# Row-group transposes, a shared PSUM pool and a VectorE finish in an attention-plus-SoLU kernel

## The chip, the core and the metric

One core of a Trainium2 chip runs the kernel. The metric is device time in microseconds (us): the median of the runs, 1267.34 us before (three runs, 1265.64 to 1268.81). The engines are TensorE (PE, its weight loads PEld), VectorE (DVE), ScalarE (ACT), GpSimd (POOL) and SyncE (SP), which issues every DMA here. All arithmetic is fp32.

## The reference

`x` is 4 batches of 12608 tokens with 128 channels; 32 learned "inducing" points attend to it, and then the tokens attend to the result. The attention output goes token by token through a feed-forward layer of width 1024:

```
h   = softmax(scale * I @ x.T) @ x          # per batch: [32,128], pass 1
y   = softmax(scale * x @ h.T) @ h          # per batch: [12608,128], pass 2
u   = y @ w_in                              # [tokens,1024]
s   = u * softmax(u)                        # "SoLU"
out = ((s - mean(s)) / sqrt(var(s) + 1e-6) * g_ln) @ w_out
```

## The kernel before, in words

Tokens are cut into tiles of 128: 99 per batch, 396 in all. Three stages run per batch.

- **Pass 1** (`p1`, L529): groups of up to 12 tiles (`PG`, nine groups a batch) are loaded, transposed on PE (`turn4`, L571, in two halves per group), copied to `xT` by ACT (L557), stored to DRAM as `xd`, scored against the inducing points (L600), reduced and exponentiated, and gathered (L682). Batch 0 does this up front with PSUM banks of its own; the next batch's pass 1 is woven into the current batch's tiles.
- **Pass 2** (`p2`, L763): groups of up to 12 tiles (`AG`) are read back from `xd`, scored (L790), transposed by DVE (L797), reduced (L799), shifted on POOL (L802), exponentiated on ACT (L809) and copied once more on POOL (L810), so that the weights stand twice. They are summed (L814), negated on ACT (L815) and inverted (L816). PE turns the doubled weights, two tiles to a transpose (`turn4`, L826), and ACT copies them to `aT` (L834).
- **Feed-forward**, tile by tile (`main` L903, `soft` L952): `mm1` (L924) multiplies the weights of one tile by `hs` = h @ w_in; DVE normalises with the row extreme (L962); ACT takes the exponential (L972); POOL multiplies (L976); ACT squares with a sum (L987); DVE transposes 32x32 blocks into `vt` (L1000). When the four tiles of a group are turned, `products` (L1034) starts two streams of 32 steps (L1045).

A 32-row matmul uses one of four row groups of the array. `mm1` of tile `i` uses the pair of row groups `i % 2`, and a products stream `w` uses pair `w`. `beats` (L855) interleaves them: while one pair does `mm1`, the other takes steps of its stream. Transposes and scores use the whole array.

Each products stream fills a PSUM buffer `op` of its own (`OP[w]`, one per pair); `evacuate` (L1059) copies it to `raw` on DVE or ACT, whichever the planner takes (L1067). Everything else shares two buffers `H`. Per three groups (`FG`) `finish` (L1076) forms the variance and its inverse root: a square on ACT (L1088), three small POOL operations (L1091 to L1093), Ln and Exp on ACT (L1098, L1099), four small POOL operations (L1104 to L1107), and per group a scaling of `raw` into `os` on ACT (L1122, four instructions) or POOL (L1118), then the store (`stored`, L1129). `floor` (L1012) prepares each group's epsilon with two POOL operations (L1017, L1018) and deals it out by DMAs.

The order on every engine is fixed when the program is built. A `Planner` (L125) runs the stages as coroutines with an estimated cost for each operation and semaphore; an engine takes, among the operations ready within `SLACK`, the one with the lowest priority number, mostly the tile index `t` plus an offset (`PR_*`). A `Lock` (L112) hands out buffers.

Of the kernel before, what the change touches and what calls it, by code (L numbers as in the profile page):

```python
# [8 lines left out]
F32 = mybir.dt.float32  # L9
# [14 lines left out]
KC = FF // P  # L24
GS = 4
FG = 3
PG = 12
AG = 12
JB = FF // M
JC = 2  # L30
BEAT = 225
EAGER = 120
# [19 lines left out]
SPARES = 8  # L52
H_LAST = -30
HN_MORE = 4
# [4 lines left out]
P1_FROM = 5  # L59
P1_GO = -20  # L60
P1_STEP = 7
P2_AHEAD = 35
P2_START = 35
PR_EX = -4
PR_EV = -20
PR_FI = 20
PR_G2 = 4
PR_HN = 2
PR_MU = 1
PR_SQ = 1  # L70
PR_TU = 6
RUSH = -100.0
SLACK = {"PE": 0, "ACT": 200, "DVE": 300, "POOL": 0, "SP": 0}
SPARE = 150
WARM = 32
WOUT = -13.5
# [169 lines left out]
def set_attention_then_solu_kernel(ctx: ExitStack, tc: tile.TileContext, x, inducing, w_in, w_out, g_ln, out):  # L246
# [6 lines left out]
    p1_groups = cut(NT, PG, GS)  # L253
# [4 lines left out]
    NP, NG = len(p1_groups), len(ff_groups)  # L258
# [26 lines left out]
    def small(i, **widths):  # L285
# [20 lines left out]
    OP = [Lock(), Lock()]  # L306
# [3 lines left out]
    A4 = Lock([buf([P, AG * 2 * M], "a4")])  # L310
# [3 lines left out]
    os_b = bufs(2, [P, GS, C], "os")  # L314
    OS = Lock()
    ST = Lock([
        dict(qe=buf([P, GS, 2], f"qe{i}"), S=buf([P, GS], f"st{i}"), dd=dd_pool.tile([P * 2 * GS], F32, name=f"dd{i}")) for i in range(4)
# [9 lines left out]
    RUN = [dict(m=buf([P, NP], f"m{i}"), l=buf([P, NP], f"l{i}"), acc=buf([P, C], f"acc{i}")) for i in range(2)]  # L327
# [118 lines left out]
    def weights_out():  # L446
# [29 lines left out]
        for k in range(NP):  # L476
            yield p1_done[0][k]
# [38 lines left out]
    p1_done, l_done = ([[Event() for _ in range(NP)] for _ in range(NB)] for _ in range(2))  # L516
    chain = [[Event() for _ in range(NP + 1)] for _ in range(NB)]
    each = PG * C
    wc_flat = wc.rearrange("p j d -> p (j d)")
    EARLY_X = Lock([f[:, i * each : (i + 1) * each].rearrange("p (s c) -> p s c", c=C) for f, n in ((wc_flat, 2), (spare, SPARES * FF // each)) for i in range(n)] + xn_b)  # L520
    EARLY_T = Lock([vt_all[:, i * each : (i + 1) * each].rearrange("p (s t) -> p s t", t=P) for i in range(3 * GS * FF // each)] + [xT_b])
    e2 = [wc_flat[:, 2 * each : 2 * each + PG * M], wc_flat[:, 2 * each + PG * M : 2 * each + 2 * PG * M]] + [o.rearrange("p s c -> p (s c)")[:, : PG * M] for o in os_b]
    EARLY_EW = Lock([(e2[i], e2[i + 1].rearrange("p (s m) -> p s m", m=M)) for i in (0, 2)] + [ew_b])
# [3 lines left out]
    turned = [Event() for _ in range(NP)]  # L527

    def p1(b, k):  # L529
        s0, n = p1_groups[k]  # L530
# [34 lines left out]
        for c0 in range(0, n, most):  # L565
# [28 lines left out]
        sc = big[:, : PG * M]  # L594
        mq = big[:, 512 - C : 512 - C + 4]
# [121 lines left out]
    def combine(b):  # L717
        prev = yield l_done[b][NP - 1]
        mine = RUN[b % 2]
        l, acc = mine["l"][:, NP - 1 : NP], mine["acc"]  # L720
# [7 lines left out]
        prev = yield p1_done[b][NP - 1]  # L728
# [27 lines left out]
        for k in range(1 if b else 2):  # L756
            spawn(half(FF if b else 512), PRIO_P1(b, NP - 1) if b else -28)
# [5 lines left out]
    def p2(b, j):  # L763
# [4 lines left out]
        for k, (g0, gn) in enumerate(p1_groups):  # L768
# [39 lines left out]
        a2 = a4.rearrange("p (s r m) -> p s r m", r=2, m=M)  # L808
        de = yield Op("ACT", 90 + 27 * n, lambda: nc.scalar.activation(a2[:, :n, 0, :], s2[:, :n, :], AF.Exp, scale=scale), d, arel)  # L809
        dp = yield Op("POOL", 100 + 30 * n, lambda: nc.gpsimd.tensor_copy(a2[:, :n, 1, :], a2[:, :n, 0, :]), de)  # L810
# [3 lines left out]
        d = yield Op("DVE", 66 + 33.4 * n, lambda: nc.vector.tensor_reduce(out=nr[:, :n], in_=a2[:, :n, 0, :], op=ALU.add, axis=AX.X), de)  # L814
        d = yield Op("ACT", 100, lambda: nc.scalar.activation(nr[:, :n], nr[:, :n], AF.Copy, scale=-1.0, bias=-1e-9), d)  # L815
        dr = yield Op("DVE", 138, lambda: nc.vector.reciprocal(rn[:, :n], nr[:, :n]), d, rel)  # L816
        give(S2, (s2, mx, nr), dr)
        for q0 in range(0, -(-n // 2), 8):
            q1 = min(q0 + 8, -(-n // 2))
            tr, trel = yield bank  # L820
            wide = min(P, (n - 2 * (q1 - 1)) * 2 * M)

            def turn4():
                for q in range(q0, q1):
                    h = P if q < q1 - 1 else wide
                    nc.tensor.transpose(out=tr[:h, (q - q0) * P : (q - q0 + 1) * P], in_=a4[:, q * P : q * P + h], identity=ident)  # L826

            dt = yield Op("PE", SWITCH + 108.7 * (q1 - q0), turn4, dp, trel)
            dc = []
            for h, qa, qb in ((P, q0, q1 if wide == P else q1 - 1), (2 * M, q1 if wide == P else q1 - 1, q1)):  # L830
                if qb > qa:
                    d = yield Op(
                        "ACT", 94 + 96 * (qb - qa),
                        lambda: nc.scalar.copy(  # L834
                            aT[:h, qa:qb, :], tr[:h, (qa - q0) * P : (qb - q0) * P].rearrange("p (q t) -> p q t", t=P)
# [5 lines left out]
            for s in range(2 * q0, min(2 * q1, n)):  # L841
                plan.set(aT_ready[(b, s0 + s)], dr, *dc)
# [399 lines left out]
```

## Time and profile before

| | |
|---|---|
| runs | 1267.34, 1268.81, 1265.64 us |
| profiled execution, first to last instruction | 1265.6 us |
| TensorE clock granted, mean | 0.988 |
| DVE, ACT, POOL busy over the span | 89%, 90%, 87% |
| DMA queue 1 (all dynamic DMAs) | 28.1% of 16 engines, 108.62 MB |
| instructions | 75903 |

The span of the profiled execution equals the fastest of the runs and lies 1.7 us below their median. In the profile a line such as `L976 POOL TENSOR_TENSOR eu<-spare,eu` is a group of instructions by source line, engine and operand names; `x187` counts them, then come busy us and mean ns of one, then the idle time just before them. `PE` rows overlap: several 32-row matmuls are in the array at once, so 98% busy does not mean that all four row groups work. A windows row gives each engine's busy us and instruction count in a stretch.

### The profile page before, as it was taken

What the parts mean: (1) busy time and instruction counts of PE and PEld (TensorE: products, weight loads), DVE (VectorE), ACT (ScalarE), POOL (GpSimd) and SP (SyncE); (2) the same over time, 40 slices, a digit from 0 to 9 for tenths busy, and PEclk for the clock granted to TensorE, in tenths of its full rate; (3) what the DMA queues carried; (4) which work ended last, traced back from release to release, by engine and by line L of the source; (5) the groups of instructions that cost most, each with busy time, mean ns of one, the idle gap of its engine ahead of it and who ended that gap; (6) DMA issues with size and microseconds to landing.
All of it is one profiled execution on the core that took longest, in us unless ns stands there. A gap on an engine that the chain in (4) does not pass through costs nothing. (4 is left out here: it accounts for less than half of the span.)

```text
span 1265.6 us, 75903 instructions
## 1 busy us (share of the span) xinstructions
PE 1236.0 (98%) x34240; PEld 1127.8 (89%) x34240; DVE 1123.3 (89%) x1803; ACT 1141.3 (90%) x2402; POOL 1100.9 (87%) x977
## 2 busy tenths in 40 slices
PE   9889999999999999999999999999999999999996
PEld 7768888899998888898999898899899999999996
DVE  5679999899988998898999999988899899999992
ACT  6379999889998999999999999899999999999994
POOL 3478888888999889898999898878899999999995
PEclk9979999999999999999999999999999999999998
DMA  9662433311133323321213325321232211111111
GB/s 358 195 168 80 129 119 104 108 52 54 30 104 110 115 93 128 113 74 44 73 52 112 110 79 158 108 68 46 59 105 54 60 48 53 47 45 29 30 30 42
DMA packets 118149, 113.48 MB, mean 90 GB/s; under 512 B 76576, under 2 KB 83776, under 8 KB 117696
## 3 DMA queue, kind: packets, MB, share of 16 engines
q1 hardware_dynamic: 117824, 108.62, 28.1%
q8 instruction: 268, 4.39, 1.4%
q14 instruction: 57, 0.47, 0.1%
HBM read 54.30 MB, written 52.18 MB: 84 GB/s over the span
## 5 line engine op out<-in xcount | busy, mean ns | idle before, releaser
L1045 PE MATMUL op<-wc,vt 32*128 32x129 f32 (+1 forms) x25600 | 1000.0, 274 | 6.6 <-issue 2.9
L1045 PEld LDWEIGHTS op<-wc,vt 32*128 32x128 f32 (+1 forms) x25600 | 944.3, 185 | 59.1 <-issue 44.3
L976 POOL TENSOR_TENSOR eu<-spare,eu 128x1024 f32<-128x1024 f32 x187 | 442.2, 2373 | 37.5 <-ACT eu L972 37.3
L924 PE MATMUL h<-hs,aT 32*128 32x128 f32 x6336 | 432.0, 275 | 6.4 <-DVE spare L962 3.2
L1000 DVE STREAM_TRANSPOSE vt<-eu 128x1024 f32<-128x1024 f32 x330 | 406.6, 1236 | 27.8 <-POOL eu L976 26.5
L924 PEld LDWEIGHTS h<-hs,aT 32*128 32x128 f32 x6336 | 389.4, 188 | 21.4 <-DVE spare L962 5.9
L987 ACT ACTIVATE sq<-eu 128x1024 bf16<-128x1024 f32 x330 | 347.0, 1051 | 39.9 <-POOL eu L976 33.4
L976 POOL TENSOR_TENSOR eu<-hn,eu 128x1024 f32<-128x1024 f32 x143 | 338.3, 2374 | 30.8 <-ACT eu L972 28.3
L962 DVE TENSOR_SCALAR_CACHE_REDUCE spare<-h,rn 128x1024 f32<-128x1024 f32 x226 | 283.1, 1257 | 24.0 <-PE h L924 19.8
L962 DVE TENSOR_SCALAR_CACHE_REDUCE hn<-h,rn 128x1024 f32<-128x1024 f32 x170 | 213.4, 1258 | 15.8 <-PE h L924 13.6
L972 ACT ACTIVATE eu<-spare,nm 128x1024 f32<-128x1024 f32 x187 | 213.5, 1142 | 7.1 <-DVE spare L962 6.8
L972 ACT ACTIVATE eu<-hn,nm 128x1024 f32<-128x1024 f32 x143 | 163.0, 1141 | 2.8 <-DVE hn L962 2.4
L976 POOL TENSOR_TENSOR spare<-spare 128x1024 f32<-128x1024 f32 x39 | 92.6, 2375 | 3.9 <-ACT spare L972 3.9
L1122 ACT ACTIVATE os<-spare,fin 128x128 f32<-128x128 f32 (+1 forms) x288 | 90.4, 390 | 2.7 <-POOL fin L1107 2.3
L1000 DVE STREAM_TRANSPOSE vt<-spare 128x1024 f32<-128x1024 f32 x66 | 81.7, 1237 | 6.4 <-POOL spare L976 5.9
L987 ACT ACTIVATE sq<-spare 128x1024 bf16<-128x1024 f32 x66 | 69.4, 1051 | 7.3 <-POOL spare L976 5.9
L976 POOL TENSOR_TENSOR spare<-hn,spare 128x1024 f32<-128x1024 f32 x27 | 64.1, 2374 | 7.1 <-ACT spare L972 7.1
L987 ACT ACTIVATION_READ_ACCUMULATOR sq<-eu 128x1 f32 x330 | 62.5, 190 | 0.0
L1067 DVE COPY spare<-op 128x258 f32<-128x258 f32 (+1 forms) x100 | 40.9, 414 | 19.4 <-PE op L1045 18.2
L972 ACT ACTIVATE spare<-spare,nm 128x1024 f32<-128x1024 f32 x39 | 44.5, 1142 | 2.8 <-DVE spare L962 2.8
L571 PE MATMUL h<-ident,xn 128*128 128x128 f32 x297 | 44.3, 283 | 0.3 <-ACT aT L834 0.3
L1067 ACT COPY spare<-op 128x258 f32<-128x258 f32 (+1 forms) x100 | 35.8, 363 | 8.7 <-PE op L1045 6.7
(166 smaller groups left out, 1010.0 us busy)
## 6 DMA issues: line engine op xcount, KB each, us to landing
out_dram<-os SPq DMA_DIRECT2D x96, 256.0 KB, 2.6
xT<-xd SPq DMA_DIRECT2D x27, 768.0 KB, 4.9
xn<-in_x_dram SPq DMA_DIRECT2D x21, 768.0 KB, 4.9
xd<-xT SPq DMA_DIRECT2D x21, 768.0 KB, 4.2
dl<-dd SPq DMA_DIRECT2D x396, 1.0 KB, 2.6
xd<-vt SPq DMA_DIRECT2D x7, 768.0 KB, 11.1
spare<-in_x_dram SPq DMA_DIRECT2D x5, 768.0 KB, 12.8
xT<-xd SPq DMA_DIRECT2D x5, 512.0 KB, 4.3
```

What stands on the lines that cost most here:

```text
L571: nc.tensor.transpose(out=tr[:, (s - c0) * P : (s - c0 + 1) * P], in_=xn[:, s, :], identity=ident)
L924: nc.tensor.matmul(hp[:, cols], lhsT=aT[rows, i // 2, :], rhs=hs[rows, cols], start=True, stop=True)
L962: lambda: nc.vector.tensor_scalar(out=hn, in0=hp, scalar1=rn, scalar2=None, op0=ALU.mult, op1=ALU.min, accum_out=nm),
L972: "ACT", 1133, lambda: nc.scalar.activation(e, hn, AF.Exp, bias=nm, scale=-1.0, accum_out=G["S"][:, s : s + 1]), d, rel, srel,
L976: d = yield Op("POOL", 2330, lambda: nc.gpsimd.tensor_tensor(out=e, in0=hn, in1=e, op=ALU.mult), de, prio=t + PR_MU)
L987: "ACT", 1040, lambda: nc.scalar.activation(sq, e, AF.Square, scale=1.0 / 32.0, accum_out=G["qe"][:, s, 0:1]), d,
L1000: lambda: nc.vector.transpose(out=G["vtb"][:, : n * FF].rearrange("p (j s t) -> p j s t", j=M, s=n)[:, :, s, :], in_=e.rearrange("p (a f) ...
L1045: nc.tensor.matmul(op[:rows, a - 2 * w, : C + 1], lhsT=vt[q, k, :], rhs=wc[q, k, :], start=(k == 0), stop=(k == JB - 1))
L1067: return lambda: eng(F["raw"][:rows, i0 : i0 + 2, :], op[:rows, :, : C + 1])
L1122: nc.scalar.activation(os[:rows, q, :], raw[:, q, :], AF.Copy, scale=y[:, i0 + q : i0 + q + 1])
```

## The change

- Groups: pass 2 takes 16 tiles (`AG`), pass 1 of batches 1 to 3 takes 16 (`PG`; batch 0 keeps 12 as `PG0`), so seven groups a batch where there were nine.
- Transposes of x (batches 1 to 3) and of the pass-2 weights go by row groups: 32 rows at a time on one pair, inside `beats`, with products steps on the other pair. The pair is chosen by which stream has nothing ready (`load`).
- The exponential writes the doubled weights itself; the copy L810 goes. The negation L815 moves from ACT to DVE.
- `mm1` takes, among the next three tiles, one whose opposite stream has steps; at most two `mm1` buffers are out at a time (`TURN`).
- PSUM: one pool of four `H` buffers; a products stream takes one of them, and `PAIR[w]` is released when its last step is issued, not when the buffer is evacuated.
- `finish` runs per five groups; its small operations run on DVE (eight), with Ln and Exp on ACT as before. `floor`'s two operations move into it. The scaling is done by POOL alone, in place in `raw`; `raw` is released when the stores are done.
- Several priorities and slacks change; there is one `hn` buffer less in the spare space.

```diff
-FG = 3
-PG = 12
-AG = 12
+FG = 5
+PG = 16
+PG0 = 12
+AG = 16
-JC = 2
+JC = 1
-EAGER = 120
+EAGER = 300
-HN_MORE = 4
+HN_MORE = 3
-P1_STEP = 7
+P1_STEP = 11
-PR_FI = 20
+PR_FI = 40
-SLACK = {"PE": 0, "ACT": 200, "DVE": 300, "POOL": 0, "SP": 0}
+SLACK = {"PE": 0, "ACT": 200, "DVE": 100, "POOL": 100, "SP": 0}
+WINDOW_TILES = 3
+MINE = 2
...
+        def by_rows(ways):
+            tr, trel = yield ltr
+            op = Op("PE", BEAT * -(-n // 2), None, [d for d, at in xd], trel, prio=RUSH)
...
+                w = min(ways, key=lambda w: (load(w) > 0, w))
...
+                def two(i):
+                    for s in range(2 * i, min(2 * i + 2, n)):
+                        for k in range(2):
+                            r = slice((2 * w + k) * M, (2 * w + k + 1) * M)
+                            nc.tensor.transpose(out=tr[:, k * 512 + s * M : k * 512 + (s + 1) * M], in_=xn[r, s, :], identity=ident[r, r])
+
+                beats(-(-n // 2), (1 - w,), two)
...
+        twice = s2[:, :n, None, :].to_broadcast([P, n, 2, M])
+        de = yield Op("ACT", 90 + 54 * n, lambda: nc.scalar.activation(a4[:, :n], twice, AF.Exp, scale=scale), d, arel)
...
+            "DVE", 75,
+            lambda: nc.vector.tensor_scalar(out=nr[:, :n], in0=nr[:, :n], scalar1=-1.0, scalar2=-1e-9, op0=ALU.mult, op1=ALU.add),
...
+    def load(w):
+        p = stream[w]
+        return JB - p["j"] if p["j"] < JB and p["ready"] <= plan.now + EAGER else 0
...
+                        s = min(near, key=lambda s: (load(slot(s) % 2) > 0, s))
...
-        op, rel = yield OP[w]
+        yield PAIR[w].at(t)
+        bank, rel = yield H.at(OP_FIRST + t)
...
+            give(PAIR[w], None)
...
-        give(OP[w], op, d)
+        give(H, bank, d)
...
+        def small(fn, *after):
+            return Op("DVE", 75, fn, *after)
+
+        de = yield small(lambda: ts(out=z, in0=S, scalar1=1e-3, scalar2=1e-12, op0=ALU.mult, op1=ALU.add), fd)
+        de = yield small(lambda: tt(out=z, in0=z, in1=z, op=ALU.mult), de)
+        d = yield small(lambda: stt(out=part, in0=total, scalar=1.0 / (FF * FF), in1=total, op0=ALU.mult, op1=ALU.mult), F["out"])
+        d = yield small(lambda: tt(out=v, in0=Q, in1=part, op=ALU.subtract), fd, d)
+        d = yield small(lambda: stt(out=v, in0=v, scalar=0.0, in1=z, op0=ALU.max, op1=ALU.add), d, de)
...
+        d = yield small(lambda: stt(out=z, in0=root, scalar=-0.5, in1=root, op0=ALU.mult, op1=ALU.mult), da)
+        d = yield small(lambda: tt(out=z, in0=z, in1=v, op=ALU.mult), d)
+        dy = yield small(lambda: stt(out=y, in0=z, scalar=1.5, in1=root, op0=ALU.add, op1=ALU.mult), d, da)
...
-            done = yield Op("ACT", 1170, scaled_act, dy, rel, alt=Op("POOL", 1000, scaled, dy, rel))
+            done = yield Op("POOL", 1000, scaled(nc.gpsimd), dy, prio=OS_PRIO)
...
-        for i in range(2):
+        for i in range(4):
             give(H, buf([P, FF], f"h{i}", where=late), *done)
```

More of the change, by code (lines that the diff above doesn't have):

```diff
@@ L475, in weights_out @@
         give(H, mp, d)
-        for k in range(NP):
+        for k in range(NP[0]):
             yield p1_done[0][k]
@@ L813, in p2 @@
         A["left"] = n
[L814 to L819, printed above, removed]
-            tr, trel = yield bank
[L821 to L828, printed above, removed]
+        pairs = -(-n // 2)
@@ new lines, in p2, with turned_rows, turn, two @@
+        ways, copied, read = [0, 1], [], []
+        def turned_rows():
+            tr, trel = yield bank
+            op = Op("PE", BEAT * -(-pairs // 2), None, de, trel)
+            got = []
+            def turn():
+                w = min(ways, key=lambda w: (load(w) > 0, w))
+                ways.remove(w)
+                got.append(w)
+                def two(i):
+                    for q in range(2 * i, min(2 * i + 2, pairs)):
+                        for k in range(2):
+                            r = slice((2 * w + k) * M, (2 * w + k + 1) * M)
+                            both = a4[r, 2 * q : min(2 * q + 2, n)].rearrange("t s r m -> t (s r m)")
+                            h = both.shape[1]
+                            nc.tensor.transpose(out=tr[:h, k * 512 + q * M : k * 512 + (q + 1) * M], in_=both, identity=ident[r, r])
+                beats(-(-pairs // 2), (1 - w,), two)
+            op.fn = turn
+            dt = yield op
+            closing(dt)
+            read.append(dt)
+            w = got[0]
@@ L965, in soft @@
         give(H, hp, d)
+        give(TURN, None, d)
         A["left"] -= 1
@@ L1085, in finish @@
         part, v, y, root, z = (F[k][:rows, :w] for k in ("part", "v", "y", "root", "z"))
-        Q, ep = (F["dl"][:rows, :w, i] for i in range(2))
-        gt, gs = nc.gpsimd.tensor_tensor, nc.gpsimd.tensor_scalar
-        d = yield Op("ACT", 110, lambda: nc.scalar.activation(part, F["raw"][:rows, :w, C], AF.Square, scale=1.0 / FF), F["out"])
-        def variance():
-            gt(out=v, in0=Q, in1=part, op=ALU.subtract)
-            gs(out=v, in0=v, scalar1=0.0, scalar2=None, op0=ALU.max)
-            gt(out=v, in0=v, in1=ep, op=ALU.add)
-        d = yield Op("POOL", 760, variance, fd, d)
+        Q, S = (F["dl"][:rows, :w, i] for i in range(2))
+        tt, ts, stt = nc.vector.tensor_tensor, nc.vector.tensor_scalar, nc.vector.scalar_tensor_tensor
+        total = F["raw"][:rows, :w, C]
+        def small(fn, *after):
[5 more added lines that the diff above has]
+        d = yield small(lambda: stt(out=v, in0=v, scalar=0.0, in1=z, op0=ALU.max, op1=ALU.add), d, de)
         def inverse():
@@ L1149, in stored @@
                     x += width
-        give(OS, os, d)
+        F["kept"].append(d)
+        if len(F["kept"]) == min(FG, NG - f * FG):
+            give(FIN, F["mine"], *F["kept"])
     for b in range(NB):
-        for k in range(NP):
+        for k in range(NP[b]):
             xd_done[(b, k)] = Event()
@@ L1168, in handover @@
         done = []
-        for k in range(NP):
+        for k in range(NP[0]):
             d = yield p1_done[0][k]
@@ L1207, in set_attention_then_solu_kernel @@
     spawn(points(), -40)
-    for k in range(NP):
+    for k in range(NP[0]):
         spawn(p1(0, k), PRIO_P1(0, k))
```

244 lines of the change are left out of this document (138 added, 106 removed).

## The prediction

> **What bounds the kernel now.** I read the busy shares first, then the windows view by stage, then the groups by line.
>
> ```profile
> span 1265.6 us, 75903 instructions
> PE 1236.0 (98%) x34240; PEld 1127.8 (89%) x34240; DVE 1123.3 (89%) x1803; ACT 1141.3 (90%) x2402; POOL 1100.9 (87%) x977
> ```
>
> Four engines stand at 87% or more, so relieving one is worth only the distance to the next. Next comes the stretch in which all the multiplies L976 lie, 60 to 1246 us, with 19.6 us behind it. Then two stretches inside it, with pass 1 and without, the second pair of rows being L976 alone.
>
> ```profile
> 60.00:1246.00 1186.00, 1170.44 (x33313) 1074.41 (x33315) 1083.98 (x1686) 1106.78 (x2315) 1074.01 (x931) 0.99 0.27 81
> ...
> 400.00:600.00 200.00, 199.12 (x5502) 178.23 (x5501) 181.57 (x308) 186.96 (x391) 173.03 (x149) 1.00 0.30 91
> 1000.00:1200.00 200.00, 198.06 (x6131) 191.28 (x6133) 190.31 (x267) 196.28 (x417) 196.18 (x174) 1.00 0.16 41
> ...
> 400.00:600.00 200.00, 151.55 (x65) 1.00 0.30 91
> 1000.00:1200.00 200.00, 174.15 (x75) 1.00 0.16 41
> ```
>
> The columns are PE, PEld, DVE, ACT, POOL. Beside pass 1, 151.55 us of multiplies at 2.373 us (row below) are 63.9 tiles, 3.13 us each; without it 73.4 tiles, 2.73 us each. In the latter POOL is 98.1% busy and sets the pace; that 98.1% is what I take as the best a bounding engine reaches. Beside pass 1 POOL has 13% to spare, DVE 9%, and only PE has nothing. So PE bounds three quarters of the stretch. But its busy time hides half-empty work:
>
> ```profile
> L1045 PE MATMUL op<-wc,vt 32*128 32x129 f32 (+1 forms) x25600 | 1000.0, 274 | 6.6 <-issue 2.9
> L924 PE MATMUL h<-hs,aT 32*128 32x128 f32 x6336 | 432.0, 275 | 6.4 <-DVE spare L962 3.2
> ...
> 385.29 0.28 PE L924 MATMUL h<-hs,aT 32*128 32x128 f32 x2
> 385.50 0.87 PE L571 MATMUL h<-ident,xn 128*128 128x128 f32 x6
> 386.31 0.47 PE L1045 MATMUL op<-wc,vt 32*96 32x129 f32 x8
> ...
> 1084.00:1088.00 4.00, 4.00 (x152) 1.00 0.03 5
> 1090.90:1092.40 1.50, 1.48 (x32) 1.00 0.12 12
> ```
>
> When both pairs work, as from 1084 to 1088, 152 instructions pass in 4 us, some eight of them counted at both edges: 36 a microsecond. At 1090.9 to 1092.4, where the trace has two products buffers evacuated, 32 pass in 1.5 us, 21 a microsecond, and PE still reads busy. The 31,936 products and `mm1` instructions (some 31,600 inside the stretch) need 31,600 / 36 = 878 us at full rate.
>
> ```profile
> L571 PE MATMUL h<-ident,xn 128*128 128x128 f32 x297 | 44.3, 283 | 0.3 <-ACT aT L834 0.3
> L826 PE MATMUL h<-ident,a 128*128 128x128 f32 x200 | 30.8, 288 | 1.7 <-DVE hn L470 1.7
> L790 PE MATMUL h<-xT,h 128*32 128x384 f32 (+3 forms) x328 | 30.4, 451 | 2.0 <-DMA xT<-xd 2.0
> L682 PE MATMUL h<-xn,ew 128*32 128x128 f32 x594 | 22.0, 277 | 0.3 <-ACT xT L557 0.3
> L600 PE MATMUL h<-xT,indT 128*32 128x384 f32 (+3 forms) x216 | 21.5, 470 | 0.0
> ```
>
> A block of six L571 transposes costs 386.31 - 385.29 - 0.11 = 0.91 us: 0.12 each ((0.87 - 0.27) / 5) and 0.19 for changing over and back. 297 of them in 54 blocks make 46 us, L826's 200 in 37 blocks 31. The other three rows are 74. 878 + 46 + 31 + 74 = 1029, so of 1186 us some 157 went to pairs with nothing to do, and a little to smaller matmuls.
>
> **The change, PE.** Turning by row groups takes beats of one pair: pass 1 has 50 beats per pair and batch (8 for a group of 16, 6 and 4 for the rest), two pairs, three batches, 300; pass 2 has 25 per pair and batch, 200 over four. If the other pair always has products steps, 500 beats of eight instructions with one half theirs cost 250 x 8 / 36 = 56 us instead of 46 + 31. That operation isn't in the trace. Bounds: 56, and 112 when nothing runs beside it; I take 56, since `load` picks the pair whose own stream is empty. Groups fall from 37 to 29 and from 27 to 21, which saves 8 + 3 x 6 change-overs of 0.19: 74 becomes 69. The 157 us of idle pairs lie between 0 and 157 afterwards: the evacuation no longer holds the pair, but streams still end unevenly. I take half, 78. PE: 878 + 56 + 69 + 78 = 1081 us, 105 less than now. It stops being the bound.
>
> **POOL and ACT.**
>
> ```profile
> 0.00:1266.00 1266.00, 112.86 (x396) 83.47 (x280) 0.99 0.30 90
> ...
> 0.00:1266.00 1266.00, 40.23 (x200) 0.99 0.30 90
> ...
> L976 POOL TENSOR_TENSOR eu<-spare,eu 128x1024 f32<-128x1024 f32 x187 | 442.2, 2373 | 37.5 <-ACT eu L972 37.3
> L1118 POOL TENSOR_TENSOR os<-spare,fin 128x512 f32<-128x512 f32 (+1 forms) x28 | 29.2, 1044 | 0.4
> L810 POOL COPY a<-a 128x384 f32<-128x384 f32 (+3 forms) x37 | 17.5, 472 | 5.6 <-ACT a L809 5.5
> L1122 ACT ACTIVATE os<-spare,fin 128x128 f32<-128x128 f32 (+1 forms) x288 | 90.4, 390 | 2.7 <-POOL fin L1107 2.3
> L809 ACT ACTIVATE a<-s 128x384 f32<-128x384 f32 (+3 forms) x37 | 18.0, 487 | 1.9 <-POOL s L802 1.9
> ```
>
> The first row is everything on the finish tiles (ACT, then POOL), the second the `floor` operations. POOL loses 40.2, the finish's small ones 83.5 - 29.2 = 54.3, and 17.5; it gains the 72 scalings that ACT did, 72 x 1.044 = 75.2: 1074 becomes 1037. ACT loses 90.4 and the short L1088 and L815 and gains at most 18 for the exponential of doubled width: 1107 becomes about 1030, plus evacuations. Neither binds: 1037 / 0.981 = 1057.
>
> **DVE** is next.
>
> ```profile
> L641 DVE TENSOR_SCALAR small<-m 128x1 f32<-128x1 f32 x36 | 5.5, 154 | 1.3
> L1067 DVE COPY spare<-op 128x258 f32<-128x258 f32 (+1 forms) x100 | 40.9, 414 | 19.4 <-PE op L1045 18.2
> ```
>
> Eight small operations for each of 20 finishes and one for each of 29 pass-2 groups, at L641's 154 ns: 24.6 + 4.5. Six pass-1 groups less save about 6. With ACT relieved, more evacuations go there: between 0 and 40.9, taken as 20. 1084 + 24.6 + 4.5 - 6 - 20 = 1087, and 1108 at 98.1%, more than any other engine needs. To this comes a wait of unknown size, because the operations stand beside POOL's multiplies:
>
> ```profile
> 282.78 2.06 DVE L729 TENSOR_SCALAR accn<-acc,small 128x128 f32<-128x128 f32 x1
> 282.40 2.35 POOL L976 TENSOR_TENSOR eu<-hn,eu 128x1024 f32<-128x1024 f32 x1
> 588.52 0.29 DVE L729 TENSOR_SCALAR accn<-acc,small 128x128 f32<-128x128 f32 x1
> 15.79 1.22 DVE L418 SCALAR_TENSOR_TENSOR eu<-eu 128x1024 uint32<-128x1024 uint32 x1
> 16.37 0.86 POOL L660 TENSOR_SCALAR l<-l,small 128x1 f32<-128x1 f32 x1 [1.84 <-ACT os L651]
> L660 POOL TENSOR_SCALAR l<-l,small x7: 335/347/1518, 16.4 to 842.6; 128x1 f32<-128x1 f32 x7
> ```
>
> L729 takes 0.29 us, but 2.06 when it begins 0.38 us into a multiply: it ends at 284.84, 0.09 after the multiply (284.75). And POOL's L660, 0.347 us at the median, took 0.86 beside L418, a VectorE operation on two SBUF tensors, ending 0.22 after it. Seven of the eight small operations read two SBUF tensors, 140 in all. None like them runs beside a multiply in this trace, so the price of one lies between 0 and a whole multiply. I place it by where they will stand: their priority is 20 tiles late (`PR_EV` + `PR_FI` = +20), so the planner puts most where DVE has nothing better.
>
> ```profile
> DVE vt L1000 <- POOL eu L976: 26.5, 34, 2.1
> DVE spare L962 <- PE h L924: 19.8, 33, 2.2
> DVE spare L1067 <- PE op L1045: 18.2, 22, 7.8
> DVE hn L962 <- PE h L924: 13.6, 20, 1.6
> DVE vt L1000 <- POOL spare L976: 5.9, 11, 1.2
> ```
>
> Of these 84 us of DVE's gaps 32.4 (39%) end with a multiply; an operation held there costs nothing more. The others wait for PE, 51.6 us in 75 gaps, 0.69 each: beyond such a gap the rest of a multiply met at random is (2.373 - 0.69)^2 / (2 x 2.373) = 0.60 us, times 0.9 for POOL's share. 140 x 61% x 0.54 = 46 us. DVE: 1087 + 46 = 1133, at 98.1% 1155 us.
>
> **The end.**
>
> ```profile
> 1259.46 1.04 POOL L1118 TENSOR_TENSOR os<-spare,fin 96x512 f32<-96x512 f32 x1
> ```
>
> The last finish now has five groups where 25 groups by threes left one: four more scalings in series behind the last evacuation, +4.2 us, with nothing to cover them.
>
> At nothing: the hn buffer less (L962's gaps above end with PE, not with a free buffer); `raw` kept until its stores land (its next use is 20 tiles away); SP, which issues no DMA more. If that cover goes, rival C has the price.
>
> **Sum.** Stretch 1186 to 1155, -31; end +4: 1265.6 - 27 = 1239 on the profiled execution. That lies 1.7 under the median of the runs, so **1241**.
>
> **Rivals.**
> A. The small operations don't wait at all (the L418 row is for 1024 columns of another type; here there are 20). Then DVE needs 1108, -78 + 4: 1193, with the 1.7, **1194**. For it: no row shows a short two-tensor operation held. Against: L729 is short and was held.
>
> B. Every one waits, wherever it stands, since `finish` is late when DVE is full: half a multiply times 0.9, 1.07 us x 140 = 149. DVE: 1236 / 0.981 = 1260, +74 + 4: **1346**, slower. It decides against the change from 72 us of waiting on, 0.51 us an operation, where 1087 + 72 fills the 1182 us that the stretch may take. [...]
>
> C. PE stays the bound: four buffers shared by two streams, `mm1` and both passes run out (as when `raw` is not back and an evacuated stream's buffer stands), so that the 157 us stay, and turning finds no steps beside it, 112. 878 + 112 + 69 + 157 = 1216: +30 + 4, **1301**. Against: it needs both at once; with one alone PE needs 1160 or 1137, at or below the forecast's 1155.
>
> **Chances.** Forecast 0.45 (its own range 1215 to 1262: waits of 21 to 67 us in place of 46), A 0.22, B 0.22, C 0.11. A measurement of this kernel tells about 0.3% from no change, 4 us. Faster: 0.43 + 0.22 + 0.03 (C with one half of it) = 0.68; same: 0.02 + 0.02 + 0.04 = 0.08; slower 0.24. The range: 1190, just under A, to 1305, just over C; what it leaves out is B's upper part (0.15) and a little under A.
>
> **What would show it.** Right: in the windows with pass 1, DVE rises to 96% or more and a tile takes less than 3 us; L571 and L826 are gone as blocks, and products rows lie between 32-row transposes at about 36 instructions a microsecond; the finish operations that stand before `vt` L1000 end with a multiply. A would show them at 0.1 to 0.2 us throughout; B at over 1 us on the mean, DVE full, POOL and PE idle behind it; C, PE full below 30 instructions a microsecond. The forecast is wrong if DVE stays below 93% in the stretch, or the finish operations together take much other than 46 + 25 us.

## The result and the profile after

The changed kernel takes 1383.04 us (four runs, 1374.45 to 1387.33) against 1268.07 for the kernel before (four runs): ratio 1.0892, 95% interval 1.0852 to 1.0931. The forecast of 1241 was wrong in size and in sign, and the time lies 78 us above its range. The profile is that of the slowest of the four runs, 1387.33. The page of the changed kernel, to be read beside the first fence of the prediction:

```profile
span 1385.1 us, 77913 instructions
PE 1236.7 (89%) x35557; PEld 1142.9 (83%) x35557; DVE 1255.2 (91%) x1882; ACT 1062.2 (77%) x2015; POOL 1072.8 (77%) x557
```

PE is no longer full, its busy time is as before (1236.7 us for 1236.0), and the only engine with clearly more busy time is DVE: 1255.2 us where it had 1123.3. The windows view of the same kernel gives the stretch that holds all the multiplies (the last ends at 1351.55) and the two inner stretches, then the multiplies L1069 alone (columns PE, PEld, DVE, ACT, POOL, then clock, DMA share, GB/s):

```profile
60.00:1351.60 1291.60, 1163.85 (x34442) 1082.65 (x34440) 1209.31 (x1743) 1026.84 (x1930) 1040.29 (x518) 0.95 0.25 72
400.00:600.00 200.00, 181.47 (x5397) 166.66 (x5400) 183.68 (x283) 155.79 (x292) 160.23 (x80) 0.97 0.32 98
1000.00:1200.00 200.00, 178.11 (x5356) 169.17 (x5356) 192.58 (x254) 157.11 (x298) 167.24 (x84) 0.96 0.21 55
...
400.00:600.00 200.00, 142.67 (x61) 0.97 0.32 98
1000.00:1200.00 200.00, 146.43 (x63) 0.96 0.21 55
```

142.67 us are 60 tiles beside pass 1, where before had 64, and 62 without it, where before had 73. DVE is 92% busy beside pass 1 and 96% without; it is the busiest in both. What it does there shows in the groups by line (count, then busy us and mean ns of one):

```profile
L911 DVE TENSOR_SCALAR nr<-nr 128x16 f32<-128x16 f32 (+3 forms) x29 | 55.2, 1905 | 0.1
L1185 DVE TENSOR_SCALAR fin<-dl 128x20 f32<-128x20 f32 x20 | 26.1, 1305 | 0.3 <-issue 0.3
L1186 DVE TENSOR_TENSOR fin<-fin 128x20 f32<-128x20 f32 x20 | 24.1, 1207 | 0.2
L1189 DVE SCALAR_TENSOR_TENSOR fin<-fin 128x20 f32<-128x20 f32 x20 | 15.6, 781 | 0.3
L1188 DVE TENSOR_TENSOR fin<-dl,fin 128x20 f32<-128x20 f32 x20 | 14.7, 734 | 0.3
L1187 DVE SCALAR_TENSOR_TENSOR fin<-spare 128x20 f32<-128x20 f32 x20 | 11.4, 571 | 0.0
L1196 DVE SCALAR_TENSOR_TENSOR fin<-fin 128x20 f32<-128x20 f32 x20 | 11.1, 553 | 0.5 <-ACT fin L1193 0.5
L1198 DVE SCALAR_TENSOR_TENSOR fin<-fin 128x20 f32<-128x20 f32 x20 | 9.4, 469 | 0.2
L1197 DVE TENSOR_TENSOR fin<-fin 128x20 f32<-128x20 f32 x20 | 9.0, 449 | 0.1
...
L914 DVE RECIPROCAL rn<-nr 128x16 f32<-128x16 f32 (+3 forms) x29 | 6.3, 218 | 0.1
```

The first nine rows are the 29 negations and the 160 operations of `finish`: 176.6 us, where the forecast had 75 (24.6 + 4.5 + 46). Of the 189, 83 took over 0.4 us, 158.9 us together, and every one of these begins while a multiply runs and ends 0.03 to 0.06 us after a multiply ends; the others took 0.17 on the mean. The 87 that begin outside a multiply took at most 0.19. I call an operation that waits in this way held. The last row, one tensor of the same 16 columns three lines below the negation, is never held: 19 of the 29 begin while a multiply runs, and the longest took 0.25. One line at the end of the program shows both cases, beside the last multiplies (which end at 1351.55) and after them:

```profile
1343.95 7.63 DVE L1185 TENSOR_SCALAR fin<-dl 128x20 f32<-128x20 f32 x1
...
1372.65 0.18 DVE L1185 TENSOR_SCALAR fin<-dl 128x20 f32<-128x20 f32 x1
```

The timeline shows how far a hold can go:

```profile
860.19 4.70 POOL L1069 TENSOR_TENSOR eu<-spare,eu 128x1024 f32<-128x1024 f32 x2
862.99 8.84 DVE L911 TENSOR_SCALAR nr<-nr 128x16 f32<-128x16 f32 x1
864.85 6.95 POOL L1069 TENSOR_TENSOR eu<-hn,eu 128x1024 f32<-128x1024 f32 x3
871.74 1.27 DVE L1054 TENSOR_SCALAR_CACHE_REDUCE spare<-h,rn 128x1024 f32<-128x1024 f32 x1
```

The second multiply of the first row runs from about 862.52 (860.19 + 4.70 - 2.37). The negation of 16 columns begins 0.47 us into it and is let go at 871.83, after that multiply and three more (864.85 + 6.95 = 871.80). For 8.84 us DVE does nothing else. Five operations were held through more than one multiply, 4.6 to 9.14 us; all five are `tensor_scalar` (L911 and L1185), and each was let in only where GpSimd paused for 0.46 us or more. No operation with two tensors took longer than 2.40. In the view of waits the other engines stand behind DVE:

```profile
POOL eu L1069 <- ACT eu L1065: 131.5, 60, 6.6
ACT spare L1159 <- PE h L1136: 111.6, 65, 11.2
PEld h L1013 <- DVE spare L1054: 53.5, 25, 8.0
PE h L1013 <- DVE spare L1054: 46.6, 21, 7.8
```

`mm1` (L1013) waits for the normalising on DVE to free its PSUM buffer, up to 8.0 us. The first row was 65.6 us before and the second, evacuations on ACT that wait for a late PE, 6.7; the last two are new at this size (the normalising before cost `mm1` 3.2 us on PE).

### The profile page after: what moved, and what is told of

The parts are those of the page before. It is cut to its first block, busy times and chain, and to the rows that moved or that the text cites. A ratio compares the mean times of both kernels' runs of the same rounds, so it can differ in the third digit from the quotient of the medians.

```text
span 1385.1 us, 77913 instructions
## 1 busy us (share of the span) xinstructions
PE 1236.7 (89%) x35557; PEld 1142.9 (83%) x35557; DVE 1255.2 (91%) x1882; ACT 1062.2 (77%) x2015; POOL 1072.8 (77%) x557
## 5 line engine op out<-in xcount | busy, mean ns | idle before, releaser
L1136 PE MATMUL h<-wc,vt 32*128 32x129 f32 x25600 | 1068.9, 280 | 34.0 <-issue 17.1
L1136 PEld LDWEIGHTS h<-wc,vt 32*128 32x128 f32 x25600 | 1023.8, 191 | 71.3 <-issue 40.5
L1013 PE MATMUL h<-hs,aT 32*128 32x128 f32 x6336 | 459.6, 286 | 81.0 <-DVE spare L1054 46.6
L1069 POOL TENSOR_TENSOR eu<-hn,eu 128x1024 f32<-128x1024 f32 x197 | 463.3, 2372 | 77.4 <-ACT eu L1065 75.5
L1013 PEld LDWEIGHTS h<-hs,aT 32*128 32x128 f32 x6336 | 408.0, 196 | 109.1 <-DVE spare L1054 53.5
L1069 POOL TENSOR_TENSOR eu<-spare,eu 128x1024 f32<-128x1024 f32 x133 | 313.7, 2375 | 58.8 <-ACT eu L1065 56.0
L1054 DVE TENSOR_SCALAR_CACHE_REDUCE hn<-h,rn 128x1024 f32<-128x1024 f32 x198 | 248.6, 1261 | 29.7 <-PE h L1013 20.5
L1054 DVE TENSOR_SCALAR_CACHE_REDUCE spare<-h,rn 128x1024 f32<-128x1024 f32 x198 | 248.8, 1260 | 25.8 <-PE h L1013 23.2
L1065 ACT ACTIVATE eu<-hn,nm 128x1024 f32<-128x1024 f32 x197 | 224.9, 1143 | 25.4 <-DVE hn L1054 19.6
L1069 POOL TENSOR_TENSOR spare<-spare 128x1024 f32<-128x1024 f32 x65 | 154.2, 2372 | 31.6 <-ACT spare L1065 31.4
L1065 ACT ACTIVATE eu<-spare,nm 128x1024 f32<-128x1024 f32 x133 | 151.9, 1143 | 24.8 <-DVE spare L1054 20.4
L1205 POOL TENSOR_TENSOR spare<-spare,fin 128x512 f32<-128x512 f32 x100 | 101.0, 1042 | 46.7 <-issue 32.1
L1159 ACT COPY spare<-h 128x258 f32<-128x258 f32 (+1 forms) x119 | 43.7, 371 | 112.1 <-PE h L1136 111.6
L583 PE MATMUL h<-ident,xn 32*128 32x32 f32 x1188 | 54.3, 227 | 6.6 <-DVE spare L1054 3.7
```

The costliest lines, as they stand in the source:

```text
L583: nc.tensor.transpose(out=tr[:, k * 512 + s * M : k * 512 + (s + 1) * M], in_=xn[r, s, :], identity=ident[r, r])
L1013: nc.tensor.matmul(hp[:, cols], lhsT=aT[rows, i // 2, :], rhs=hs[rows, cols], start=True, stop=True)
L1054: lambda: nc.vector.tensor_scalar(out=hn, in0=hp, scalar1=rn, scalar2=None, op0=ALU.mult, op1=ALU.min, accum_out=nm),
L1065: "ACT", 1133, lambda: nc.scalar.activation(e, hn, AF.Exp, bias=nm, scale=-1.0, accum_out=G["qe"][:, s, 1:2]), d, rel, srel,
L1069: d = yield Op("POOL", 2330, lambda: nc.gpsimd.tensor_tensor(out=e, in0=hn, in1=e, op=ALU.mult), de, prio=t + PR_MU)
L1136: nc.tensor.matmul(op[:rows, a - 2 * w, : C + 1], lhsT=vt[q, k, :], rhs=wc[q, k, :], start=(k == 0), stop=(k == JB - 1))
```

## Experiments: the small operations

The theory after the result: the small operations on DVE, held behind POOL's multiplies, cost all of the loss. The rival: the rest of the change costs it (PSUM pool, turns, order). Each ratio below is to the kernel before on the same chip; the batches ran on different chips, so runs of two batches are compared by their ratios.

**e1_small_off_dve**, after with the nine kinds elsewhere:

```
-        de = yield small(lambda: ts(out=z, in0=S, ...))      # and seven more, DVE
+        de = yield Op("POOL", 500, floors, fd)               # and variance, newton on POOL, the square on ACT
-        d = yield Op("DVE", 75, lambda: nc.vector.tensor_scalar(out=nr[:, :n], ...), d)
+        d = yield Op("ACT", 100, lambda: nc.scalar.activation(nr[:, :n], nr[:, :n], AF.Copy, scale=-1.0, bias=-1e-9), d)
```

> The changed kernel with the nine kinds of short operations taken off VectorE again: the finish's eight go to GpSimd (nine short ones there, and a square on ScalarE), the negation of the sums to ScalarE. Everything else of the change stays. Theory (VectorE held by GpSimd's multiplies): the 177 us that these operations took on VectorE go, VectorE needs about 1050 us of the stretch and nothing is held, so 1195 to 1235 us. Rival (the other parts of the change cost the time: one pool of PSUM buffers, row-group turns, later priorities): above 1330 us.

1267.05 us, ratio to before 0.9998 (0.997 to 1.0026), above the 1195 to 1235 expected. Its windows row:

```profile
60.00:1239.70 1179.70, 1139.98 (x34581) 1069.21 (x34584) 1055.50 (x1573) 1031.55 (x1983) 1074.09 (x684) 0.98 0.28 79
```

DVE does 154 us less in the stretch and the time falls by 116: without these operations on DVE the loss is gone. The granted clock, 0.95 in this stretch of after, is 0.98 here (0.99 in before). But the forecast's gain isn't there either. With none of them held, the rest of the change is worth nothing, though GpSimd does 34 us more here than in after, and no engine in this row is over 97%.

**e2_negation_on_act** moves the negation alone (the second hunk above).

> The changed kernel with one instruction per pass-2 group moved, 29 in all: the negation of the sums goes back to ScalarE. Theory: these 29 took 55 us on VectorE, three of them 7 to 9 us each, which also emptied the buffers behind; 1315 to 1335 us. Rival: 29 instructions of 16 columns weigh nothing, 1375 to 1390 us.

1363.51 us, ratio 1.0753 (1.072 to 1.0786): between the two expectations. 55 us of negations gone saved 20, because another operation is now held for longer:

```profile
L1181 DVE TENSOR_SCALAR fin<-dl 128x20 f32<-128x20 f32 x20 | 46.4, 2321 | 0.2
L1182 DVE TENSOR_TENSOR fin<-fin 128x20 f32<-128x20 f32 x20 | 15.2, 759 | 0.2
```

The first operation of `finish` (L1185 in after, 26.1 us there) went from 1305 to 2321 ns, its longest from 7.63 to 8.67 us. Again five operations, all of this `tensor_scalar`, were held through several multiplies until GpSimd paused. So the cost of the same operation depends on the line of multiplies that it meets.

**e3_one_tensor** is e2 with the eight operations of `finish` replaced in their places by `nc.vector.reciprocal` of one tensor.

> The changed kernel with the negation on ScalarE and each of the finish's eight VectorE operations replaced by a reciprocal of one of its inputs: the same number, the same tiles written, the same place in the order, but one SBUF tensor read instead of two. It leaves out the finish's arithmetic. Theory (it is the form that is held, not the number or the place): as fast as the kernel with the operations off VectorE plus some 20 us of its own time at most, 1200 to 1250 us, each operation at 0.15 to 0.22 us. Rival (160 dependent short operations in VectorE's order cost whatever their form): within 15 us of the kernel with only the negation moved.

1257.8 us, ratio 0.9908 (0.9887 to 0.993), 8 us above the expectation. All eight rows lie between these two, 0.23 to 0.27 us an operation:

```profile
L1185 DVE RECIPROCAL fin<-fin 128x20 f32<-128x20 f32 x20 | 5.3, 265 | 0.3
L1183 DVE RECIPROCAL fin<-spare 128x20 f32<-128x20 f32 x20 | 4.7, 233 | 0.0
```

Same engine, number, place and columns: 106 us less than e2. 122 of the 160 begin while a multiply runs, and the longest took 0.28. It is the form of the operation that costs, not the place or the count. The number of columns is part of the form, as a line of the kernel before shows:

```profile
L641 DVE TENSOR_SCALAR small<-m x36: 153/154/156, 13.0 to 893.7; 128x1 f32<-128x1 f32 x36
```

This is a `tensor_scalar` of one column (the three figures are its least, median and longest ns). 21 of the 36 begin while a multiply runs, and none is held, where L911 in after is held with 7 columns as with 16.

**e4_before_small_on_dve** gives the kernel before six of these operations per finish, 36 finishes, and nothing else of the change.

```
-        d = yield Op("POOL", 760, variance, fd, d)
+        d = yield small(lambda: tt(out=v, in0=Q, in1=part, op=ALU.subtract), fd, d)      # and five more on DVE
```

> The kernel before with one part of the change alone: the finish's short operations on VectorE, six for each of 36 finishes, all of them reading two SBUF tensors. Theory: 216 at the mean of 0.68 us that the two-tensor ones took in the changed kernel, 147 us, against some 100 us that VectorE had idle: 1300 to 1350 us. Rival (these operations hide in VectorE's gaps): 1260 to 1272 us.

1390.19 us, ratio 1.096 (1.0931 to 1.099), beyond the expectation. The dearest and the cheapest of the six:

```profile
L1095 DVE TENSOR_TENSOR fin<-dl,fin 128x12 f32<-128x12 f32 (+1 forms) x36 | 46.4, 1289 | 4.4 <-DMA dl<-dd 2.2 <-DVE fin L1094 0.8 <-DMA dd<-qe 0.2
...
L1105 DVE SCALAR_TENSOR_TENSOR fin<-fin 128x12 f32<-128x12 f32 (+1 forms) x36 | 6.4, 177 | 1.2
```

Together they are 141 us (147 expected) and cost 122. All 70 that begin while a multiply runs end after it. So the held operations alone are enough for the loss, and in e1 their absence is enough to undo it.

## Experiments: where the gain went

Four variants of e1, each with one part put back as before (e5: partly):

**e5_small_off_scale_act**: `done = yield Op("ACT", 1170, scaled_act, ..., alt=Op("POOL", 1000, ...))`.

> e1 (small operations off VectorE) with the scaling of raw free to go to ScalarE as before (four instructions a group) or to GpSimd. What is open after e1 and e3 is where the 70 us went that PE should have gained. Theory P (GpSimd): e1 has GpSimd at 1074 of 1180 us, 91%, and at 94 to 97% from 900 to 1200 us; the scalings that moved there (75 us) took the gain. Then moving about half of them to ScalarE (1032 of 1180 us busy) gives 1230 to 1245. Theory S (no engine is full; each stands in its fixed order behind the next one's late work): within 1% of e1, 1255 to 1275.

**e6_own_buffers**: `bank, rel = yield OP[w]` in place of `yield H.at(OP_FIRST + t)`, released by the evacuation.

> e1 with the PSUM of the kernel before: two buffers for everything else and one buffer for each pair's products stream, held until it is evacuated. My prediction credited the pool of four with 78 us of idle pairs; e1 shows 151 us of idle pairs where before had 127. Theory U (the pool and the early release are worth nothing here, a stream waits for its vt blocks or its order and not for its buffer): within 1% of e1, 1255 to 1275. Rival V (the pool does its 78 us of good, and something else in the change costs as much): 1320 to 1350. Rival W (the pool itself costs: a turn that holds a buffer for eight beats, and two mm1 at most): 1220 to 1250.

**e7_settings_before**: `SLACK`, `PR_EX`, `PR_FI`, `PR_HN`, `PR_TU`, `EAGER`, `JC`, `WOUT` of the kernel before.

> e1 with the planner's settings of the kernel before (slack of VectorE 300 and GpSimd 0, priorities of normalising, exponential, turning and finish, products two steps at a time, eager 120). Theory S (the order is what holds e1 back: evacuations on ScalarE and VectorE stand up to 7.5 us in order for a late PE, 61 us in the two groups where before had 25): the settings move the time by over 1%, either way. Rival (the settings are neutral, buffers or GpSimd decide): 1260 to 1275.

**e8_full_turns**: `nc.tensor.transpose(out=tr[:, ...], in_=xn[:, s, :], identity=ident)` in blocks of eight, for x and the weights.

> e1 with x and the weights turned on the whole array again, in blocks of eight between the products, groups of 16 kept. Costed as in the prediction: row turns took 77 us of interruptions away and cost 56, so this should be 21 us slower than e1 where PE sets the pace, 1280 to 1295. Theory S (PE isn't what sets the pace in e1): within 0.7% of e1, 1258 to 1276. Rival (the turns by rows hold their buffer and their pair longer than they save): 1235 to 1255.

| run | us | ratio to before, interval |
|---|---|---|
| e1 (from the first batch) | 1267.05 | 0.9998 (0.997 to 1.0026) |
| e5 | 1258.85 | 0.9909 (0.9887 to 0.9932) |
| e6 | 1269.36 | 1.0001 (0.9971 to 1.003) |
| e7 | 1290.74 | 1.0169 (1.0139 to 1.02) |
| e8 | 1267.05 | 0.998 (0.9962 to 0.9999) |

e5, e6 and e8 came out within 1% of e1, as their theory S or U had it; e7 moved by over 1%. The pool of PSUM buffers and the turns by row groups (the transposes of the change), which the forecast credited with most of PE's gain, make no difference that can be measured. Scaling on GpSimd alone cost 0.7 to 0.9% (e1 to e5, by time and by ratio), not the 2 to 3 that theory P expected. The settings are worth 1.7%. e5 is also the version that beats both kernels, by 0.9% and by 9%. The groups of 16, the five groups to a finish and the choice among three tiles were not put back alone.

**e11_before_settings_after** asks whether those settings are good in themselves.

> The kernel before with the planner's settings of after (slack of VectorE and GpSimd 100, priorities, eager 300, one products step at a time), nothing else. e7 showed that the settings are worth 1.7% in e1, so that the parts of the change without them would stand 1.7% behind the kernel before. If the settings are good for any version: 1240 to 1255. Rival (they fit the changed kernel only, as a planner's settings do): 1268 to 1300.

1326.89 us, ratio 1.0453 (1.0406 to 1.05), beyond the rival's 1300: no, they fit the changed kernel only. **e16_beat_235** is e5 with `BEAT = 235`.

> e5 with the planner's cost of a beat of eight PE instructions at 235 ns instead of 225; only the order changes. e10 (e1 with half of the products) came out 41 us faster than e1, e9 9 us faster than before: in the changed kernel the engines stand more behind a PE that is later than its place in the order, at a granted clock of 0.97 where before had 0.99. If the order counts on a PE that is too fast, the truer cost gives 1235 to 1252. If a change of order is worth nothing: 1255 to 1265.

1268.04 us, ratio 1.0014 (0.9985 to 1.0042), outside both expectations and 0.7 to 1.1% behind e5. A slower PE in the plan doesn't help.

Then the forecast's first reading, that PE bounds three quarters of the kernel before. Six runs halve one engine's large operation in a fixed order, four in that of before, e10 and e12 in that of e1. The products keep 17 of 32 steps; the transpose (e14) and the square (e15) are cut to half of the columns like the multiply:

```
+            if k % 2 and k < JB - 1:     # e9, e10: emit(a, k)
+                return
-  nc.gpsimd.tensor_tensor(out=e, in0=hn, in1=e, op=ALU.mult)                     # e12, e13
+  nc.gpsimd.tensor_tensor(out=e[:, : FF // 2], in0=hn[:, : FF // 2], in1=e[:, : FF // 2], op=ALU.mult)
```

> The kernel before with 17 of each stream's 32 steps (every second one is left out, so about 47% of the products aren't computed); planner's order and costs unchanged, so every other instruction stands where it stood. It tests the sentence that the whole forecast rests on, that PE bounds three quarters of the stretch. As the prediction has it: PE loses about 410 us of work, the next bound is ScalarE at 1107 or VectorE at 1084, at 98.1% that is 1105 to 1130 for the stretch: 1185 to 1215. Theory S (no engine's work sets the pace, each stands in its fixed order behind another): 1235 to 1260.

> e1 with the same 17 of 32 steps. If PE still paces e1 by pairs with nothing to do (151 us counted), the next bound is GpSimd at 1074 or VectorE at 1056, at 98.1% 1077 to 1095 for the stretch: 1165 to 1185. Theory S (PE isn't what sets the pace in e1): 1235 to 1262.

> e1 with GpSimd's multiply on 512 of the 1024 columns (half of the product s = u * softmax(u) is left out); order and costs of the plan unchanged. GpSimd loses about 220 us of 1074. Theory P (GpSimd, 91% busy with 94 to 97% from 900 us on, sets the pace): the next bound is VectorE at 1056 or PE: 1185 to 1220. Theory S: 1235 to 1260, since the chain's length from a tile's exponential to its products is shorter by 1.1 us only.

> The kernel before with GpSimd's multiply on 512 of 1024 columns (half of s = u * softmax(u) is left out), order and costs of the plan unchanged. e9 took 47% of the products away and the time fell by 9 us only, so PE isn't the bound that I took it for. If GpSimd is (it is 98% busy from 1000 to 1200 us, 87% elsewhere): 1215 to 1235, the next being ScalarE at 93%. If no single engine is, as in e12: 1250 to 1265.

> The kernel before with VectorE's transposes into vt on 16 of 32 blocks after the first three groups (half of the products then read old data). VectorE loses about 235 us of 1084. If VectorE sets the pace by its place between GpSimd and PE (normalise, transpose and evacuation stand in one order there): 1190 to 1230. If no single engine does: 1250 to 1265.

> The kernel before with ScalarE's square and sum on 512 of 1024 columns (the variance is wrong by the other half). ScalarE, the busiest engine beside PE at 1107 of 1186 us, loses about 170 us. If ScalarE sets the pace: 1195 to 1235. If no single engine does: 1250 to 1265.

| halved | before: us, ratio | e1: us, ratio |
|---|---|---|
| products (PE) | 1260.5, 0.9931 (0.9907 to 0.9956) | 1225.75, 0.9652 (0.9597 to 0.9708) |
| multiply (POOL) | 1261.1, 0.9943 (0.9925 to 0.9962) | 1258.99, 0.9919 (0.9888 to 0.995) |
| transpose (DVE) | 1265.88, 0.9983 (0.9965 to 1.0001) | not run |
| square (ACT) | 1257.99, 0.993 (0.991 to 0.9949) | not run |

In the kernel before no engine's relief is worth more than 0.7%, where the prediction's reading gave PE 4 to 7% (e9). All but e10 came out within a microsecond of the ranges for "no single engine sets the pace"; e10 fell between its two expectations. Two runs then leave PE whole and halve the five large operations of all the others (normalise, exponential, multiply, square, transpose), in before and in e1:

```
+        cols = FF if t < 20 else FF // 2     # e17, e18: each of the five on [:, :cols]
```

> The kernel before with the five large operations of a tile on the other engines (normalise, exponential, multiply, square, transpose) on 512 of 1024 columns after the first 20 tiles; PE's work and the order unchanged, half of the results old or missing. Of e9, e13, e14 and e15 none alone moved the time by more than 9 us. If PE alone also fills its stretch (a second bound, level with the other three), the time stays at 1240 to 1265, and then e9 and this one together say that PE and the rest are equal bounds. If the time is in the handing over between full engines, this takes half of it away: 1100 to 1200.

> e1 with the same five operations halved after the first 20 tiles, so that PE stands alone. The forecast had PE's own need fall by 105 us (1186 to 1081 in the stretch). If it fell so and e1 stands at 1267 only because the rest (e10: 1226) and the order hold it: 100 us below e17, 1140 to 1165. If PE's need didn't fall (the idle pairs come from elsewhere than the evacuation): within 1% of e17.

1251.45 us (0.9855, 0.9821 to 0.9888) and 1247.17 us (0.9821, 0.9788 to 0.9854). The pages of e17 and of e18:

```profile
PE 1219.8 (98%) x34240; PEld 1116.4 (89%) x34240; DVE 745.0 (60%) x1803; ACT 838.4 (67%) x2402; POOL 695.9 (56%) x977
```

```profile
PE 1191.6 (96%) x35557; PEld 1112.3 (89%) x35557; DVE 721.9 (58%) x1691; ACT 755.3 (61%) x2066; POOL 704.7 (57%) x737
```

With the others little over half busy, PE in its order needs 1251 us in before and 1247 in e1. The others, with half of the products, need 1260 in before and 1226 in e1. So before reads as two level bounds, PE at 1251 and the rest at 1260, 19 and 9 us under its time (1270.19 and 1269.06 beside them). The change took 35 us off the rest and 4 off PE, which the two intervals don't tell from nothing, where the forecast took 105 off PE. No run relieves both at once, so a third limit that both pairs of runs share isn't excluded: in e17 PE is 98% busy, but in e9 the fullest of the others, ACT, is at 91%.

What PE did with the 1170 us between 60 and 1230 us, counted over the records of its instructions: products and `mm1` (and row turns) at 36 a microsecond, the time from one of them to the next wherever whole-array work lies between, less one step of 0.11, and what is left. The forecast's column is for its stretch of 1186 us.

| us | e17 (before) | e18 (e1) | forecast, before to after |
|---|---|---|---|
| products, `mm1` at full rate | 878 | 885 | 878, 878 |
| row turns | none | 55 | none, 56 |
| whole-array work between | 177 | 92 | 151, 69 |
| half-empty beats and pauses | 115 | 138 | 157, 78 |
| of these, pauses over 0.5 us that wait for no semaphore | 7 | 27 | |

The whole-array work fell as forecast, by 85 us for 82. The 55 us of the row turns are their number, 1980, at that rate, so they agree with the forecast's 56 by count only; in e18 they stand among products steps, and the stretches that hold them, 75.5 us with 1032 other instructions, are 47 us longer than those need. The idle pairs didn't fall: without the pauses they are 111 us in e18 and 108 in e17, with the other engines half idle and in e18 no stream's pair bound to its evacuation; and e6, where it is bound, is no slower than e1. The place that the prediction showed as held by two evacuations (32 instructions in 1.5 us) is, in e17's windows, little fuller with DVE nearly idle there:

```profile
1079.00:1080.50 1.50, 1.50 (x56) 1.50 (x52) 0.76 (x2) 0.12 (x1) 0.02 (x1) 1.00 0.74 156
1080.50:1082.00 1.50, 1.50 (x38) 1.50 (x36) 0.31 (x1) 0.97 (x3) 0.00 (x0) 1.00 0.72 208
1082.00:1083.50 1.50, 1.50 (x50) 1.50 (x52) 1.50 (x5) 1.29 (x4) 0.82 (x4) 1.00 0.02 0
```

38 in the middle row instead of 32, where 54 would be full. Quick evacuations don't fill the pairs; that the order itself issues one stream's steps alone there is the likely reason, which is argued and not shown.

The pauses are new at this size. The products' group in e17 and in e18:

```profile
L1046 PE MATMUL op<-wc,vt 32*128 32x129 f32 (+1 forms) x25600 | 992.3, 274 | 5.8 <-issue 5.5
```

```profile
L1133 PE MATMUL h<-wc,vt 32*128 32x129 f32 (+1 forms) x25600 | 1022.1, 275 | 26.0 <-issue 23.2 <-ACT aT L889 0.7 <-DVE vt L1090 0.6
```

"issue" is a wait for nothing that the profile shows. The longest, 3.0 us, in e18's windows (PE, PEld, DVE, ACT, POOL, clock, DMA share, GB/s):

```profile
722.00:724.00 2.00, 2.00 (x80) 2.00 (x76) 0.65 (x2) 0.99 (x4) 2.00 (x3) 1.00 0.99 358
724.00:727.30 3.30, 0.32 (x14) 0.21 (x7) 1.16 (x3) 0.00 (x0) 2.37 (x2) 1.00 0.52 127
727.30:729.30 2.00, 2.00 (x34) 2.00 (x37) 0.00 (x0) 0.46 (x2) 0.00 (x0) 0.55 0.55 99
```

The DMA engines are 99% busy, then PE stands still for most of the next 3.3 us, then it runs at a granted clock of 0.55. Of the 21 gaps in e18 of over 0.9 us from one start to the next, 16 follow two microseconds with a DMA share of 0.59 or more; the mean is 0.29. The page of e18 has a queue that bears on these gaps, and that of e10 beside it:

```profile
q8 instruction: 278, 4.55, 1.5%
```

```profile
q8 instruction: 184, 3.01, 1.0%
```

The packets are 16 KB. e18 has 35,557 multiplies and as many loads, 71,114 instructions or 278 times 256; e10 has 2 x 23,557, 184 times 256. By this count the queue carries PE's instructions, 256 to a packet, and 256 of them last 3.6 us at the 36 multiplies and 36 loads a microsecond of full rate. The records of the traces tie the pauses to it. All 23 pauses over 0.5 us in e18 in which PE waits for no semaphore, and all 7 in e17, end 1.1 to 1.6 us after a packet of this queue has landed, where a moment taken at random has one so far behind it in about one case of eight; and from each of the 23 to the next the trace has a multiple of 256 PE instructions, to within 9. So in these pauses PE, by all that the records show, waits for its own instructions. The kernel before has 3 of them, 2.9 us in all, and e1 has 18, 22.0 us: a cost to PE that the change brought. Why the packets come late is argued: groups of 16 move 1024 KB at a time where groups of 12 moved 768, and 16 of the 21 long gaps follow a DMA share of 0.59 or more, but no run changed the size of the transfers alone.

## Why the prediction was wrong

- **The wait of DVE's small operations (46 us).** This is the step that decided. It failed in three ways. It counted the 140 with two SBUF tensors and let the `tensor_scalar` ones go free: L911 and L1185 alone took 81 of 176.6 us, though the prediction's own evidence, L729, was a `tensor_scalar` of one tensor (the price of 0.154 us comes from L641, a line of one column, which is never held: 0.156 us at most). It placed the operations in DVE's gaps; the idle time before them is 0.5 us or less a group, so they stood in the full part of the order. And it took the rest of one multiply as the longest wait; five were held longer, up to 9.14 us. Against 0.17 us an operation, the 140 waited 72 us where the sum had 46, and the 49 others 73 where it had nothing. By its own sign of being wrong, the operations of `finish` took 121 us where it allowed 71.
- **Rival B** had the mechanism and, by luck, nearly its size: 149 us for waiting; measured 176.6 less 189 at the free 0.17 is 145. It had it from the 140 alone, which waited 72. That each of these waits, 1.07 us on the mean, was the author's estimate, which no row of before shows for 20 columns; in after 62 of the 140 begin inside a multiply, 49 of these took over 0.4 us, and the 140 waited 0.51 us on the mean. The one-tensor L911 is held as well, for up to 9.14 us; the normalise (L1054, `TENSOR_SCALAR_CACHE_REDUCE`) is not: it took 1.29 us at most, inside a multiply as outside. The rest of one multiply, as the longest wait, is too short by up to three multiplies for five of the 83.
- **98.1% for a bounding engine.** DVE's own sum came out: 1058 without the small operations, 1055.5 in e1, though only 9 us of evacuations left it there (40.9 to 32.2) and not 20. But the stretch is 1291.6 us for 1209.3 of DVE, 93.6%. At 98.1% it would be 1233. When DVE is held, PE and ACT wait as well: `mm1` waited 46.6 us on PE for the normalising (`PE h L1013 <- DVE spare L1054`), where it waited 3.2 before, and ACT's exponential into `eu` waited 40.0 for it, where it waited 9.2. DVE then waits for them: its normalising and evacuations waited 76 us for PE, where they waited 52 before. That is the likely reason why the time passed B's 1346.
- **PE bounds, and the evacuation holds its pairs.** PE's 105 us were the gain. Its own need fell by 4 (e17, e18). In the same 1170 us it spent 85 less between and 55 on turns, got through 7 us more of products, and spent 23 more on beats and pauses, 20 of them in the pauses that wait for no semaphore. The step that failed is "I take half, 78" of the idle pairs: 108 and 111 us without the pauses, so the evacuation wasn't what held them.
- **One bound at a time.** The prediction read 87 to 98% as four engines of which only PE counted beside pass 1. e9 shows that halving PE's products gives 0.7%: PE was not the only limit there.
- **Right:** POOL 1037 (1040.3), the turns' 56 (47 to 55), the five scalings at the end. ACT's 1030 (1026.8 in the stretch of after) is right by luck: its terms add up to 1019, and of the evacuations that it left out 8 us came to ACT (43.7 for 35.8 before). The sums of rivals A and B come out a microsecond lower than they say, 1193 and 1345. The five scalings take 5.03 us in the first row below:

```profile
1374.84 5.03 POOL L1205 TENSOR_TENSOR spare<-spare,fin 128x512 f32<-128x512 f32 x5 [13.25 <-issue]
...
1354.66 17.67 PE L1136 MATMUL h<-wc,vt 32*128 32x129 f32 x512 [6.22 <-DVE vt L1093]
```

  After the last multiply come 33.5 us where before had 19.6. 4 of the 14 are the scalings; in the second row 512 products of the last groups are still to run, where before had 308, and the forecast had no more of them.

What stays open: what makes a waiting `tensor_scalar` sit through several multiplies and others be let in after one, why PE's instructions come late, what keeps the other 111 us of PE's pairs idle, and what holds the rest of the engines, none of them full, at 1260 us in before and 1226 in e1.

## What to carry to other kernels

Before moving small work to VectorE beside a GpSimd that is busy with multiplies of two tensors (2.37 us each here), look at the form of each instruction. Price one of a form that was held here (the negation L911 and the operations of `finish`) at the whole line of GpSimd work behind which it may stand, up to 9.14 us for a `tensor_scalar` in after and 2.40 for an operation with two tensors, plus what waits for VectorE meanwhile. A form that wasn't held cost its own time: a reciprocal 0.23 to 0.27 us (e3), a `tensor_scalar` of one column 0.15 (before), the negation on ScalarE 0.21 (e2, e3). A busy share near 100% doesn't prove a bound: PE was 98% busy in before, and half of its products were worth 0.7%. Halve the work of that engine in the same order, then halve all the others, and compare the two times with the whole. In before both came within 2%, and relieving one engine alone paid 0.7% at most.

## What the runs showed of the hardware that was not expected

- In after a VectorE `tensor_scalar` of 16 columns was held through four GpSimd multiplies in a row, 8.84 us, and another took 9.14; the 106 of the 189 that took under 0.4 us took 0.17 on the mean. A reciprocal of the same columns was never held (218 ns on the mean, 0.25 us at most), nor was a `tensor_scalar` of one column in before (156 ns at most).
- PE paused for up to 3.0 us with no semaphore to wait for, 27 us in e18 and 7 in e17, each time until 1.1 to 1.6 us after a packet of queue q8 had landed, whose packets count 256 PE instructions each; the granted clock stood at 0.55 after the longest. 16 of the 21 gaps over 0.9 us in e18 follow a DMA share of 0.59 or more, where the mean is 0.29.
